# Attention with position bias and two feed-forward stages on one core: one pair of heads instead of two handled tile by tile right behind the bias rows

## The chip, the core and the metric

The kernel runs on one core of a Trainium2 chip. The metric is the time of one execution in microseconds (us) on the device. Five engines work side by side, each through its own instructions in order: TensorE (PE; its weight loads, PEld, are listed apart), VectorE (DVE), ScalarE (ACT), GpSimd (POOL) and SyncE (SP), whose queue issues nearly all DMA transfers.

## The reference

```python
scores = scale * np.matmul(q, k.transpose(0, 1, 3, 2))        # 4 batches, 8 heads, 576 tokens, head size 64
x = (np.log1p(np.abs(rel)) / psi_i)[..., None]                # rel: distance of two positions
bias = np.maximum(x @ w1 + b1, 0.0) @ w2                      # hidden size 32, one value per head
scores = scores + bias.transpose(2, 0, 1)[None]               # the same bias for every batch
attn = softmax(scores)
x = (attn @ v)                                                # to 2304 tokens x 512
h = x @ w_in; x = (P(h) / Q(h)) @ w_out                       # P, Q: polynomials; 2048 hidden
h = max(x @ w1, x @ w2, x @ w3); out = h @ w_out              # 768 hidden
```

## The kernel before, in words

The work has four stages: the bias rows, attention, and two feed-forward stages. Nearly all engines follow an order of instructions that is written out by hand (`ordered(3)` and the step list `A2` in the constants `KN`).

**Bias stage** (lines 1014 to 1037). The bias depends on the distance of two tokens, for each row divided by a number of that row. It is built in 36 groups of 16 rows: `bias_hidden` makes four hidden tiles of a group (ReLU of table plus column), each on ScalarE (line 189) or on VectorE (line 191); the list `H2` names the groups whose second hidden tile is ScalarE's. `bias_out` multiplies them on TensorE (line 215), evicts the sum on ScalarE (line 220) and stores it to DRAM (line 222). `bias_load` (lines 234 and 240 to 242) reads the rows back, skewed, for one tile of 128 query rows (t = 0 to 3, the last, t = 4, has 64) and one pair of heads (p = 0 to 3). SP's queue holds all these stores and loads in order.

In the same stage the first `FP` = 2 pairs of batch 0 are prepared: `split_kq` writes k and q as a high part and a remainder (fp32r), in six steps, placed by `SP0` behind given groups and run on VectorE. The k and q loads of pairs 0 and 1 are the first transfers of the kernel; those of pair 2 stand in the stage as well (`L0`). Bias rows of pairs below `FP` are loaded in this stage (the fifth tile's at position 2 of attention), those of the others four positions ahead of their use.

**Attention** (`attn_tick`, line 1130) works through a list of 80 units (batch, group of tiles, tile t, pair p). For a unit: scores on TensorE (line 268, or 279 for t = 4), a VectorE reduction that adds the bias and finds the maximum (line 294), exponentials with row sums on ScalarE (line 300); two positions later transposes on TensorE (lines 400, 406) and their evictions on ScalarE and VectorE (lines 1169, 421, 423); two more positions later the product with v (line 451), scaled by the reciprocal sums and stored.

The reciprocal sums take one of two ways. Pairs that are "own" (batch 0, p < `FP`) go tile by tile, in the order t0 p0, t0 p1, t1 p0, ...: each unit's sums are guarded (line 328, GpSimd), inverted (line 333, VectorE), spread over 64 columns (line 335, GpSimd) and transposed on TensorE with the unit's tiles (line 409). All other pairs go five units at a time, tiles [0, 1] and [2, 3, 4]; their sums are guarded once per group on ScalarE (line 326), inverted, and go through DRAM (lines 354 and 364). For pairs that are not own, `splits_at` puts the split's steps, two per position, on GpSimd, and `loads_at` their k and q loads. From position 10 on, feed-forward weights are brought in as well.

Of the kernel before, what the change touches and what calls it, by code (L numbers as in the profile page):

```python
# [17 lines left out]
P = 128  # L18
# [8 lines left out]
HID = 32  # L27
LR = 608
EW = S + 15
KN = {'PM': [0, 1, 2, 3, 4, 5, 6, 7, 8, 9, 10, 11, 12, 13, 14, 15, 16, 17, 18, 19, 20, 21, 22, 23, 24, 25, 26, 27, 28, 29, 30, 31, 32, 33, 34, 35], 'GD': 1, 'XS': 5, 'A3': ['na', 'T', 'v0', 'v1', 'av', 'n', 'st'], 'RL': 2, 'NSG': 4, 'RX': 2, 'AVL': 2, 'NSLOT': 35, 'NRAW': 3, 'NRAWX': 2, 'NATT': 4, 'HB': 0, 'NE': 'd', 'FP': 2, 'BL': 4, 'T4': 0, 'LSP': 1, 'KX': 2, 'HT': 'ss', 'EVP': 'da', 'TTP': 'dda', 'NXS': 5, 'EARLY': 4, 'NM0': 0, 'MAN': 3, 'MANF': 3, 'HA': 2, 'H0': [34, 35], 'L0': [(3, 'k2'), (6, 'v2')], 'B4': 2, 'H2': [1, 2, 4, 6, 8, 12], 'SP0': [3, 4], 'BW': 10, 'A2': ['na', 'sc', 'sq1', 'av', 'T', 'r0', 'r1', 'st', 'n', 'p1', 'p2', 'sq', 'e0', 'e1', 'v0', 'v1'], 'LL': 7, 'SL': 3, 'LL0': 9, 'SL0': 2, 'SQ': [1], 'CUT2': 1, 'CUT3': 4, 'WS': 14, 'WR': 41, 'EV': {None: 'da', 's': 'da', 'j': 'aa'}, 'WT': 64, 'XT': 8, 'XA': 3, 'XB': 8, 'F': ['g2a', 'g2d', 'h', 'g1a', 'w', 'g2p', 'g1d', 'g1p', 'y', 'x', 'g3'], 'LOW': 0, 'LOM': 3, 'LOI': 2, 'GHI': 'dve', 'GLO': 'dve', 'BED': 8, 'BE0': 16, 'NU1': 'pool', 'XE': ['act', 'pool'], 'RS': 3, 'PW': 1, 'WP': 10, 'NPK': 27, 'YSP': 'act', 'LAG': 2, 'EV1': 'dve', 'XSE': 'act', 'STQ': 'sp', 'PUQ': 'sp', 'NB0': 0, 'HP': 0, 'SB': 2, 'XLA': 3, 'XLB': 6, 'XSA': 11, 'YL': 4, 'MIX': [1, 2, 3], 'YN': [(6, 2), (6, 4), (6, 6), (7, 1), (7, 3), (7, 5), (8, 1), (8, 3), (8, 4), (8, 5)], 'WLOW': 1, 'YSN': {5: 2, 6: 2, 7: 1, 8: 1, 9: 1, 10: 1, 11: 1, 12: 1}, 'PLAN': [(2, 1, [0, 2, 3, 4, 5, 6, 7, 8]), (3, 1, [4, 6, 7, 8, 9, 10, 11, 12]), (4, 1, [8, 10, 11, 12, 13, 14, 15, 16]), (5, 2, [0, 2, 4, 5, 6, 8, 10, 12, 14]), (6, 3, [0, 2, 3, 4, 5, 6, 7, 8]), (7, 3, [4, 6, 7, 8, 9, 10, 11, 12]), (8, 3, [8, 10, 11, 12, 13, 14, 15, 16]), (0, 4, [0, 2, 3, 4, 5, 6, 7, 8]), (1, 4, [6, 8, 9, 10, 11, 12, 13, 14])], 'WPN': {13: 1, 14: 1, 15: 1}, 'OB': [1, 5]}  # L30
REBIAS = 2.0 ** -112
TOSIGN = -2.0 ** 32
QC = 1.0 + 1e-6
# [4 lines left out]
def tile_attention_moe(  # L38
# [7 lines left out]
    pe, act, dve, pool, sp = nc.tensor, nc.scalar, nc.vector, nc.gpsimd, nc.sync  # L46
# [5 lines left out]
    def slot(name, shape, dt):  # L52
        return sb.tile(shape, dt, tag="slot", name=name, bufs=KN['NSLOT'])

    def raw(name, shape, dt):
        return sb.tile(shape, dt, tag="raw", name=name, bufs=KN['NRAW'])

    def rawx(name, shape, dt):
        return sb.tile(shape, dt, tag="rawx", name=name, bufs=KN['NRAWX'])

# [34 lines left out]
    A0, A1, A2, A3 = (par[:, i:i + 1] for i in range(4))  # L95
# [206 lines left out]
    def own(b, p):  # L302
        return b == 0 and p < KN["FP"]
# [14 lines left out]
    def sum_guard(b, ts, t, p, eng=pool):  # L318
        if own(b, p):
            r = sums[b, t, p, 0]  # L320
        elif t == ts[-1]:
            r = sums[b, tuple(ts), p][0]
        else:
            return
        if eng is act:
            act.activation(r, r, AF.Identity, bias=eps)
        else:
            eng.tensor_scalar(r, r, 1e-9, 0.0, ALU.add, ALU.add)

    def sums_turn(b, ts, t, p):  # L330
        if own(b, p):
            r = sums.pop((b, t, p, 0))
            dve.reciprocal(r, r)
            rb = sb.tile([P, 512], F32, tag="xs", name=f"rb{b}_{t}_{p}", bufs=KN['NXS'])[:, :P].rearrange("p (u d) -> p u d", u=2)
            pool.tensor_copy(rb, r.unsqueeze(2).to_broadcast([P, 2, 64]))
            rbs[b, t, p] = rb
            return
        if t != ts[-1]:
            return
        sum_guard(b, ts, t, p, act)  # L340
        ts = tuple(ts)
        r_off.append((b, ts, p))
        r, sg = sums.pop((b, ts, p))
        dve.reciprocal(r, r)
        tr = sb.tile([P, 32], F32, tag="sgt", name=f"sgt{b}_{ts[0]}_{p}", bufs=3)
        dve.transpose(tr, sg)
        for n, t in enumerate(ts):
            for u in range(2):
                if t < 4:
                    rows = tr[2 * n + u:P:32, :]  # L350
                else:
                    rows = tr[64 * u + 2 * n:64 * u + 64:32, :]
                dst = r_d[b, p][u, t * P:min(S, (t + 1) * P)]
                r_due.append(lambda dst=dst, rows=rows: sp.dma_start(dst.rearrange("(c i) -> c i", i=32), rows))
# [609 lines left out]
    loads_at, splits_at, bloads_at = {}, {}, {}  # L964
# [4 lines left out]
    for i, (b, ts, t, p) in enumerate(units):  # L969
        if b == 0 and t == 4 and p < KN["FP"]:  # L970
            bloads_at.setdefault(KN["B4"], []).append((t, p))
        if t == 0 and (b > 0 or p >= KN["FP"]):
            lead, lag = (KN["LL0"], KN["SL0"]) if (b, p) == (0, KN["FP"]) else (KN["LL"] - 1, KN["SL"] - 1) if (b, p) == (1, 0) else (KN["LL"], KN["SL"] - 1) if b else (KN["LL"], KN["SL"])
            loads_at.setdefault(i - lead, []).append((b, p))
            splits_at.setdefault(i - lead + lag, []).append((b, p))
        if b == 0 and late(t, p):
            bloads_at.setdefault(i - KN["BL"], []).append((t, p))

# [151 lines left out]
    def attn_tick(n):  # L1130
# [7 lines left out]
        u1 = units[n - 1] if 1 <= n <= NU else None  # L1138
# [4 lines left out]
        for step in KN["A2"] if n <= NU else KN["A3"]:  # L1143
            if step == "sc" and u0:
                if u0[2] == u0[1][0]:
                    at_tiles(u0[0], u0[1], u0[3])
                    sums_begin(u0[0], tuple(u0[1]), u0[3])
                scores(u0[0], u0[2], u0[3])
            elif step in ("r0", "r1") and u0:
                reduce_min(u0[0], u0[2], u0[3], int(step[1]))  # L1150
                if step == "r1" and xlow and xlow[-1]:
                    xlow.pop()()
            elif step in ("e0", "e1") and u0 and (step == "e0" or u0[2] < 4):
                expo(u0[0], u0[2], u0[3], int(step[1]))
            elif step == "st":
                while stq:
                    attn_store(*stq.pop(0))
                stq.extend(st_next)
                st_next.clear()
            elif step == "T" and u2:  # L1160
                ev = transposes(u2[0], u2[2], u2[3], n >= NU)
            elif step == "na" and u1:
                if own(u1[0], u1[3]):
                    sum_guard(*u1)
            elif step == "n" and u1:
                sums_turn(*u1)
                tail_copy(u1[0], u1[2], u1[3])
            elif step == "v0" and u2:
                act.copy(*ev[0])  # L1169
            elif step == "v1" and u2:  # L1170
                for e_ in ev[1:len(ev) - 1]:
                    evac(evp, e_)
                evac(ttp, ev[-1])
            elif step == "p1":
                early_pop(kind)
            elif step == "av":
                if avq and avq[0][0] <= n:
                    _, av, js = avq.pop(0)
                    attn_v(*av, js)
                    if 4 in js:  # L1180
                        (st_next if len(av[1]) == 2 and not own(av[0], av[2]) else stq).append(av)
                if u2 and u2[2] == u2[1][-1]:
                    av = (u2[0], u2[1], u2[3])
                    cuts = {1: (5,), 2: (3, 2), 3: (2, 2, 1), 4: (4, 0, 1), 5: (5,)}
                    cut = {1: (5,), 2: cuts[KN["CUT2"]], 3: cuts[KN["CUT3"]]}[len(u2[1])]
                    avq.extend((n + KN["AVL"], av, range(sum(cut[:k]), sum(cut[:k + 1]))) for k in range(len(cut)))
            elif step == "sq1":
                for bp in splits_at.get(n, []):
                    sqq.extend(split_kq(*bp))
                if sqq:  # L1190
                    sqq.pop(0)()
            elif step == "sq":
                for _ in range(KN["SQ"][n % len(KN["SQ"])]):
                    if sqq:
                        sqq.pop(0)()
# [7 lines left out]
        WT, XT = KN["WT"], KN["XT"]  # L1203
# [13 lines left out]
    n = NU  # L1217
# [107 lines left out]
```

## Time and profile before

| what | us |
|---|---|
| median of three runs | 992.99 (992.95 to 995.52) |
| the profiled execution | 993.15 |
| its span, first to last instruction | 991.4 |
| bias stage, to the first scores | 53.5 |
| ten units of the two own pairs, to the third pair's first scores | 29.5 |
| busy: TensorE, VectorE, ScalarE, GpSimd | 976.3, 760.7, 636.7, 478.6 |

The granted TensorE clock is full throughout. Busy time of TensorE is counted with modelled ends of its matmuls, so weight loading (PEld) is the better sign of how full it is within a short stretch.

### The profile page before, as it was taken

To read this page: it belongs to the slowest core of one execution; us is meant where nothing else is said; L and a number is where in the kernel's file an instruction comes from. 1 tells how busy PE (TensorE), PEld (TensorE's weight loads), DVE (VectorE), ACT (ScalarE), POOL (GpSimd) and SP (SyncE) were. 2 spreads that over 40 slices of the span, in tenths; PEclk is the share of its full clock that TensorE was granted. 3 is DMA by queue.
4 is the path that set the end of the run, shared out by engine and by line. 5 is a ranking of instruction groups with operands and counts; after the bars stand their busy time and mean duration, and the time that the engine had idled before them with its cause. 6 is when DMAs were issued, how large, how long until landed. Compare 5 with 4: busy or idle time off the path is not lost. (4 is left out here: it accounts for less than half of the span.)

```text
span 991.4 us, 17489 instructions
## 1 busy us (share of the span) xinstructions
PE 976.3 (98%) x6076; PEld 813.0 (82%) x6076; DVE 760.7 (77%) x1466; ACT 636.7 (64%) x1319; POOL 478.6 (48%) x549
## 2 busy tenths in 40 slices
PE   6999999999999999999999999999999999999998
PEld 2389777787777788888898888887899999999997
DVE  8976787777687998988898888978696565666554
ACT  8977888888798888777788778788531211131111
POOL 4054766567572546256545356489431741371111
PEclk9999999999999999999999999999999999999999
DMA  8998686765662531223332332511597458655711
GB/s 312 320 301 268 237 280 208 265 221 205 191 217 92 184 102 43 75 85 138 104 121 97 116 127 96 181 61 60 198 388 249 159 192 285 225 172 200 256 32 64
DMA packets 76265, 176.69 MB, mean 178 GB/s; under 512 B 8848, under 2 KB 29968, under 8 KB 76176
## 3 DMA queue, kind: packets, MB, share of 16 engines
q1 hardware_dynamic: 76032, 175.27, 51.3%
q8 instruction: 48, 0.79, 0.3%
q14 instruction: 41, 0.34, 0.1%
q10 hardware_dynamic: 144, 0.29, 0.1%
HBM read 128.66 MB, written 46.87 MB: 177 GB/s over the span
## 5 line engine op out<-in xcount | busy, mean ns | idle before, releaser
L611 PE MATMUL y<-gs,wwo 128*128 128x512 f32 (+1 forms) x940 | 213.6, 373 | 1.1 <-POOL gs L669 0.6
L611 PE MATMUL ph<-xs,wwi 128*128 128x512 f32 (+1 forms) x930 | 205.6, 369 | 0.2
L611 PEld LDWEIGHTS y<-gs,wwo 128*128 128x128 f32 x940 | 164.2, 188 | 37.0 <-POOL gs L669 3.4
L611 PEld LDWEIGHTS ph<-xs,wwi 128*128 128x128 f32 x930 | 162.4, 188 | 32.9 <-issue 0.9
L897 PE MATMUL pr<-yo,ws 128*128 128x384 f32 x875 | 188.8, 335 | 0.4 <-ACT u L912 0.4
L669 POOL TENSOR_TENSOR gs<-gring,gs 128x512 fp32r<-128x512 f32 (+1 forms) x77 | 92.9, 1206 | 158.0 <-ACT gs L668 78.0
L897 PEld LDWEIGHTS pr<-yo,ws 128*128 128x128 f32 x875 | 155.5, 188 | 5.9 <-ACT u L912 0.7
L300 ACT ACTIVATE e<-e,st 128x576 f32<-128x576 f32 x144 | 110.9, 774 | 30.5 <-DVE st L294 29.2
L294 DVE CUSTOM_DVE_ANT_0 e<-s,bias 128x576 f32<-128x576 f32 x144 | 103.9, 752 | 27.3 <-PE s L268 13.8
L876 POOL TENSOR_TENSOR h<-m,h 128x384 fp32r<-128x384 f32 x36 | 36.5, 1015 | 157.3 <-ACT h L875 139.4
L642 ACT ACTIVATE s<-ph,keep 128x512 f32<-128x512 f32 (+1 forms) x80 | 49.5, 619 | 61.3 <-PE ph L611 60.8
L268 PE MATMUL s<-k,qs 128*128 128x288 f32 x512 | 84.8, 306 | 1.4 <-DVE st L294 0.5
L944 PE MATMUL o<-wmo,h 128*128 128x512 f32 x324 | 82.8, 393 | 0.0
L400 PE MATMUL tp<-ident,e 128*128 128x128 f32 x564 | 78.1, 279 | 0.2 <-ACT at L1169 0.2
L912 ACT COPY u<-pr 128x384 f32<-128x384 f32 x27 | 12.9, 478 | 101.4 <-PE pr L897 101.4
L400 PEld LDWEIGHTS tp<-ident,e 128*128 128x128 f32 x564 | 61.5, 141 | 19.4 <-issue 7.1
L268 PEld LDWEIGHTS s<-k,qs 128*128 128x128 f32 x512 | 70.1, 189 | 3.5 <-DVE st L294 1.8
L644 DVE SCALAR_TENSOR_TENSOR gring<-gring,keep,s 128x512 f32<-128x512 f32 (+1 forms) x77 | 53.0, 688 | 25.8 <-ACT gring L643 25.3
L451 PE MATMUL av<-at,v 128*64 128x320 f32 (+3 forms) x576 | 70.1, 385 | 0.0
L944 PEld LDWEIGHTS o<-wmo,h 128*128 128x128 f32 x324 | 60.1, 188 | 9.7
L875 ACT CAST h<-m 128x384 fp32r<-128x384 f32 x36 | 18.5, 514 | 70.7 <-DVE m L886 64.5
L656 DVE SCALAR_TENSOR_TENSOR gring<-gring,keep,s 128x512 f32<-128x512 f32 (+1 forms) x77 | 53.2, 691 | 11.8 <-ACT s L650 7.1
(174 smaller groups left out, 1862.1 us busy)
## 6 DMA issues: line engine op xcount, KB each, us to landing
ws<-ms_d SPq DMA_DIRECT2D x75, 512.0 KB
ms_d<-wring SPq DMA_DIRECT2D x21, 512.0 KB
bias_d<-bo SPq DMA_DIRECT2D x36, 295.5 KB
kr<-in_k SPq DMA_DIRECT2D x16, 576.0 KB
qr<-in_q SPq DMA_DIRECT2D x16, 576.0 KB
bias<-bias_d SPq DMA_DIRECT2D x16, 576.0 KB
nr<-in_m SPq DMA_DIRECT2D x18, 512.0 KB
wrwin<-in_wi SPq DMA_DIRECT2D x16, 512.0 KB
```

Source lines behind the costliest of these rows:

```text
L268: pe.matmul(pt[:, x, :HS], lhsT=qs[:, u, t * P:(t + 1) * P], rhs=ks[u][:, w, x * HS:(x + 1) * HS], start=w == 0, stop=w == 1,)
L294: dve.tensor_tensor_reduce(out=dst, in0=src, in1=bs, op0=ALU.add, op1=ALU.min, scale=-0.125, scalar=3.0e38, accum_out=st[:, u:u + 1],)
L300: act.activation(et[:, u], et[:, u], AF.Exp, bias=st[:, u:u + 1], scale=-1.0, accum_out=sums[b, t, p][u])
L400: pe.transpose(tp[:, j * P:(j + 1) * P], flat[:, 640 * u + j * P:640 * u + (j + 1) * P], ident)
L451: pe.matmul(po[r, :n], lhsT=l, rhs=m, start=j == 0, stop=j == 4, skip_group_check=True)
L611: pe.matmul(po, lhsT=wpart(key, a, k), rhs=rhs, start=first and i == 0, stop=last and i == 2)
L642: act.activation(s, ph, AF.Abs, scale=B0)
L644: dve.scalar_tensor_tensor(q, q, B1, s, ALU.mult, ALU.add)
L656: dve.scalar_tensor_tensor(u, u, A0, s, ALU.add, ALU.mult)
L669: (dve if blk == 0 and f < KN["GD"] else pool).tensor_tensor(t[1], u, f32(t[0]), ALU.subtract)
L897: pe.matmul(pt, lhsT=w[:, a, ch * P:ch * P + P], rhs=ys[c][ch], start=ch == 0 and i == 0, stop=ch == 1 and i == 2,)
L944: pe.matmul(po, lhsT=h[:, a, (tt % 3) * P:(tt % 3 + 1) * P], rhs=mo_t[j][:, c], start=j == 0 and i == 0, stop=j == NF2 - 1 and i == 2,)
```

## The change

`FP` goes from 2 to 1: only pair 0 of batch 0 is own, with units t0 to t4 of pair 0 first and pair 1 after it in groups [0, 1] and [2, 3, 4]. From this follows: VectorE no longer splits pair 1 in the bias stage (`SP0` has one entry); its split runs on GpSimd from position 0 on. Its bias rows are loaded four positions ahead of their use and no longer in the bias stage. Its sums go through DRAM. `H2` shrinks from six groups to three, so the second hidden tiles of groups 4, 8 and 12 pass from ScalarE to VectorE. For own units the guard and the spreading of the reciprocal pass from GpSimd to ScalarE. Pair 2's split keeps its place at position 3; pair 3's load moves from position 8 to 6 and its split from 11 to 9 (`LX`).

```diff
-KN = {... 'FP': 2, ... 'H2': [1, 2, 4, 6, 8, 12], 'SP0': [3, 4], ...}
+KN = {... 'FP': 1, ... 'H2': [1, 2, 6], 'SP0': [3], ... 'LX': 9}
...
-            pool.tensor_copy(rb, r.unsqueeze(2).to_broadcast([P, 2, 64]))
+            act.copy(rb, r.unsqueeze(2).to_broadcast([P, 2, 64]))
...
-            lead, lag = (KN["LL0"], KN["SL0"]) if (b, p) == (0, KN["FP"]) else (KN["LL"] - 1, KN["SL"] - 1) if (b, p) == (1, 0) else (KN["LL"], KN["SL"] - 1) if b else (KN["LL"], KN["SL"])
+            lead, lag = (KN["LL0"], KN["SL0"]) if (b, p) == (0, KN["FP"]) else (KN["LL"], 0) if (b, p) == (0, 2) else (KN["LX"], 3) if (b, p) == (0, 3) else (KN["LL"] - 1, KN["SL"] - 1) if (b, p) == (1, 0) else (KN["LL"], KN["SL"] - 1) if b else (KN["LL"], KN["SL"])
             loads_at.setdefault(i - lead, []).append((b, p))
-            splits_at.setdefault(i - lead + lag, []).append((b, p))
+            splits_at.setdefault(max(0, i - lead + lag), []).append((b, p))
...
                 if own(u1[0], u1[3]):
-                    sum_guard(*u1)
+                    sum_guard(*u1, act)
```

## Rows read from the trace of the kernel before

**Rows 1.** The page's engine totals: busy us, share of the span, instructions.
```profile
PE 976.3 (98%) x6076; PEld 813.0 (82%) x6076; DVE 760.7 (77%) x1466; ACT 636.7 (64%) x1319; POOL 478.6 (48%) x549
```
**Rows 2.** Busy time by stretch: stretch, length, busy per engine, clock, DMA share, GB/s.
```profile
0.00:53.40 53.40, 45.21 (x640) 17.25 (x640) 47.41 (x123) 47.12 (x77) 11.13 (x31) 1.00 0.91 322
53.40:65.10 11.70, 11.29 (x108) 9.88 (x98) 9.30 (x27) 10.57 (x26) 5.56 (x11) 1.00 0.93 337
65.10:83.00 17.90, 17.90 (x197) 16.46 (x196) 11.15 (x31) 11.20 (x27) 8.37 (x22) 1.00 0.88 265
...
128.60:144.30 15.70, 15.70 (x125) 12.52 (x124) 12.79 (x34) 13.49 (x35) 10.08 (x14) 1.00 0.82 271
```
**Rows 3.** Waits of weight loading, 10 to 53.4 us: total, times, longest.
```profile
PEld pb L215 <- ACT bo L220: 17.6, 29, 1.5
...
PEld pb L215 <- DVE h L191: 0.9, 4, 0.4
```
**Rows 4.** Timeline of the first positions: start, length, engine, line, instruction, count, idle before.
```profile
53.50 0.79 PE L268 MATMUL s<-k,qs 128*128 128x288 f32 x4
...
65.11 1.30 PE L268 MATMUL s<-k,qs 128*128 128x288 f32 x8
...
66.78 0.78 ACT L300 ACTIVATE e<-e,st 128x576 f32<-128x576 f32 x1 [1.02 <-DVE st L294]
...
83.01 1.30 PE L268 MATMUL s<-k,qs 128*128 128x288 f32 x8
```
**Rows 5.** Lines 147, 150, 141, 144 on VectorE: count, ns shortest/median/longest, starts, forms.
```profile
L147 DVE TENSOR_SCALAR k<-kr x4: 449/471/568, 10.8 to 12.8; 128x576 fp32r<-128x576 f32 x4
...
L150 DVE TENSOR_TENSOR k<-kr,k x4: 744/767/874, 14.5 to 19.5; 128x576 fp32r<-128x576 f32 x4
...
L141 DVE TENSOR_SCALAR qs<-qr x2: 679/680/681, 21.2 to 22.4; 128x1024 fp32r<-128x1024 f32 x2
...
L144 DVE TENSOR_TENSOR qs<-qr,qs x4: 689/689/690, 24.1 to 29.4; 64x512 fp32r<-64x512 f32 x4
```
**Rows 6.** Lines 189 and 191, the hidden tiles on ScalarE and on VectorE.
```profile
L189 ACT ACTIVATE h<-tab_sb,psi x39: 538/676/812, 5.1 to 48.7; 128x544 f32<-128x544 f32 x3, 128x512 f32<-128x512 f32 x3, 128x480 f32<-128x480 f32 x3, 128x448 f32<-128x448 f32 x3
...
L191 DVE TENSOR_SCALAR h<-tab_sb,psi x104: 370/432/528, 4.7 to 51.1; 128x576 f32<-128x576 f32 x7, 128x560 f32<-128x560 f32 x6, 128x528 f32<-128x528 f32 x6, 128x496 f32<-128x496 f32 x6
```
**Rows 7.** Timeline of the bias stage: two evictions with the idle time before them.
```profile
30.63 0.76 ACT L220 ACTIVATE bo<-pb,keep 128x591 f32<-128x591 f32 x1 [0.54 <-PE pb L215]
...
32.69 0.76 ACT L220 ACTIVATE bo<-pb,keep 128x591 f32<-128x591 f32 x1 [0.86 <-ACT h L189]
```
**Rows 8.** Lines 326, 333, 335, 409: the operations on the sums.
```profile
L326 ACT ACTIVATE sg<-sg,keep x5: 297/298/308, 89.6 to 121.0; 128x4 f32<-128x4 f32 x3, 128x5 f32<-128x5 f32 x2
...
L333 DVE RECIPROCAL so<-so x10: 152/158/168, 57.6 to 85.2; 128x2 f32<-128x2 f32 x8, 128x1 f32<-128x1 f32 x2
...
L335 POOL COPY rb<-so x10: 283/289/292, 57.9 to 85.5; 128x128 f32<-128x128 f32 x10
...
L409 PEld LDWEIGHTS tt<-ident,rb x10: 140/144/144, 59.3 to 86.4; 128*128 128x128 f32 x10
```
**Rows 9.** Timeline of GpSimd: an early tail of pair 0, and pair 2's split.
```profile
7.93 3.84 POOL L155 TENSOR_SCALAR qtail<-qr 128x64 fp32r<-128x64 f32 x1 [4.44 <-DMA qr<-in_q]
...
60.66 1.31 POOL L147 TENSOR_SCALAR k<-kr 128x576 fp32r<-128x576 f32 x2
...
66.61 0.24 POOL L155 TENSOR_SCALAR qtail<-qr 128x64 fp32r<-128x64 f32 x1
...
71.46 0.51 POOL L161 COPY vz<-v 64x64 f32<-64x64 f32 x2
```
**Rows 10.** Waits of SP's queue, 50 to 66 us: total, times, longest.
```profile
SPq L240 <- DMA bias_d<-bo: 4.8, 2, 4.0
```
**Rows 11.** Line 222, the stores of the bias rows, as in rows 5.
```profile
L222 SPq DMA_DIRECT2D bias_d<-bo x36: 315/320/456, 9.2 to 55.4; - x36
```
**Rows 12.** Timeline of SP: the first load of the fifth tile's bias rows.
```profile
62.42 0.70 SPq L240 DMA_DIRECT2D bias<-bias_d x1
```

More of the change, by code (lines that the diff above doesn't have):

```diff
@@ L29 @@
 EW = S + 15
-KN = {'PM': [0, 1, 2, 3, 4, 5, 6, 7, 8, 9, 10, 11, 12, 13, 14, 15, 16, 17, 18, 19, 20, 21, 22, 23, 24, 25, 26, 27, 28, 29, 30, 31, 32, 33, 34, 35], 'GD': 1, 'XS': 5, 'A3': ['na', 'T', 'v0', 'v1', 'av', 'n', 'st'], 'RL': 2, 'NSG': 4, 'RX': 2, 'AVL': 2, 'NSLOT': 35, 'NRAW': 3, 'NRAWX': 2, 'NATT': 4, 'HB': 0, 'NE': 'd', 'FP': 2, 'BL': 4, 'T4': 0, 'LSP': 1, 'KX': 2, 'HT': 'ss', 'EVP': 'da', 'TTP': 'dda', 'NXS': 5, 'EARLY': 4, 'NM0': 0, 'MAN': 3, 'MANF': 3, 'HA': 2, 'H0': [34, 35], 'L0': [(3, 'k2'), (6, 'v2')], 'B4': 2, 'H2': [1, 2, 4, 6, 8, 12], 'SP0': [3, 4], 'BW': 10, 'A2': ['na', 'sc', 'sq1', 'av', 'T', 'r0', 'r1', 'st', 'n', 'p1', 'p2', 'sq', 'e0', 'e1', 'v0', 'v1'], 'LL': 7, 'SL': 3, 'LL0': 9, 'SL0': 2, 'SQ': [1], 'CUT2': 1, 'CUT3': 4, 'WS': 14, 'WR': 41, 'EV': {None: 'da', 's': 'da', 'j': 'aa'}, 'WT': 64, 'XT': 8, 'XA': 3, 'XB': 8, 'F': ['g2a', 'g2d', 'h', 'g1a', 'w', 'g2p', 'g1d', 'g1p', 'y', 'x', 'g3'], 'LOW': 0, 'LOM': 3, 'LOI': 2, 'GHI': 'dve', 'GLO': 'dve', 'BED': 8, 'BE0': 16, 'NU1': 'pool', 'XE': ['act', 'pool'], 'RS': 3, 'PW': 1, 'WP': 10, 'NPK': 27, 'YSP': 'act', 'LAG': 2, 'EV1': 'dve', 'XSE': 'act', 'STQ': 'sp', 'PUQ': 'sp', 'NB0': 0, 'HP': 0, 'SB': 2, 'XLA': 3, 'XLB': 6, 'XSA': 11, 'YL': 4, 'MIX': [1, 2, 3], 'YN': [(6, 2), (6, 4), (6, 6), (7, 1), (7, 3), (7, 5), (8, 1), (8, 3), (8, 4), (8, 5)], 'WLOW': 1, 'YSN': {5: 2, 6: 2, 7: 1, 8: 1, 9: 1, 10: 1, 11: 1, 12: 1}, 'PLAN': [(2, 1, [0, 2, 3, 4, 5, 6, 7, 8]), (3, 1, [4, 6, 7, 8, 9, 10, 11, 12]), (4, 1, [8, 10, 11, 12, 13, 14, 15, 16]), (5, 2, [0, 2, 4, 5, 6, 8, 10, 12, 14]), (6, 3, [0, 2, 3, 4, 5, 6, 7, 8]), (7, 3, [4, 6, 7, 8, 9, 10, 11, 12]), (8, 3, [8, 10, 11, 12, 13, 14, 15, 16]), (0, 4, [0, 2, 3, 4, 5, 6, 7, 8]), (1, 4, [6, 8, 9, 10, 11, 12, 13, 14])], 'WPN': {13: 1, 14: 1, 15: 1}, 'OB': [1, 5]}
@@ new lines @@
+KN = {'PM': [0, 1, 2, 3, 4, 5, 6, 7, 8, 9, 10, 11, 12, 13, 14, 15, 16, 17, 18, 19, 20, 21, 22, 23, 24, 25, 26, 27, 28, 29, 30, 31, 32, 33, 34, 35], 'GD': 1, 'XS': 5, 'A3': ['na', 'T', 'v0', 'v1', 'av', 'n', 'st'], 'RL': 2, 'NSG': 4, 'RX': 2, 'AVL': 2, 'NSLOT': 35, 'NRAW': 3, 'NRAWX': 2, 'NATT': 4, 'HB': 0, 'NE': 'd', 'FP': 1, 'BL': 4, 'T4': 0, 'LSP': 1, 'KX': 2, 'HT': 'ss', 'EVP': 'da', 'TTP': 'dda', 'NXS': 5, 'EARLY': 4, 'NM0': 0, 'MAN': 3, 'MANF': 3, 'HA': 2, 'H0': [34, 35], 'L0': [(3, 'k2'), (6, 'v2')], 'B4': 2, 'H2': [1, 2, 6], 'SP0': [3], 'BW': 10, 'A2': ['na', 'sc', 'sq1', 'av', 'T', 'r0', 'r1', 'st', 'n', 'p1', 'p2', 'sq', 'e0', 'e1', 'v0', 'v1'], 'LL': 7, 'SL': 3, 'LL0': 9, 'SL0': 2, 'SQ': [1], 'CUT2': 1, 'CUT3': 4, 'WS': 14, 'WR': 41, 'EV': {None: 'da', 's': 'da', 'j': 'aa'}, 'WT': 64, 'XT': 8, 'XA': 3, 'XB': 8, 'F': ['g2a', 'g2d', 'h', 'g1a', 'w', 'g2p', 'g1d', 'g1p', 'y', 'x', 'g3'], 'LOW': 0, 'LOM': 3, 'LOI': 2, 'GHI': 'dve', 'GLO': 'dve', 'BED': 8, 'BE0': 16, 'NU1': 'pool', 'XE': ['act', 'pool'], 'RS': 3, 'PW': 1, 'WP': 10, 'NPK': 27, 'YSP': 'act', 'LAG': 2, 'EV1': 'dve', 'XSE': 'act', 'STQ': 'sp', 'PUQ': 'sp', 'NB0': 0, 'HP': 0, 'SB': 2, 'XLA': 3, 'XLB': 6, 'XSA': 11, 'YL': 4, 'MIX': [1, 2, 3], 'YN': [(6, 2), (6, 4), (6, 6), (7, 1), (7, 3), (7, 5), (8, 1), (8, 3), (8, 4), (8, 5)], 'WLOW': 1, 'YSN': {5: 2, 6: 2, 7: 1, 8: 1, 9: 1, 10: 1, 11: 1, 12: 1}, 'PLAN': [(2, 1, [0, 2, 3, 4, 5, 6, 7, 8]), (3, 1, [4, 6, 7, 8, 9, 10, 11, 12]), (4, 1, [8, 10, 11, 12, 13, 14, 15, 16]), (5, 2, [0, 2, 4, 5, 6, 8, 10, 12, 14]), (6, 3, [0, 2, 3, 4, 5, 6, 7, 8]), (7, 3, [4, 6, 7, 8, 9, 10, 11, 12]), (8, 3, [8, 10, 11, 12, 13, 14, 15, 16]), (0, 4, [0, 2, 3, 4, 5, 6, 7, 8]), (1, 4, [6, 8, 9, 10, 11, 12, 13, 14])], 'WPN': {13: 1, 14: 1, 15: 1}, 'OB': [1, 5], 'LX': 9}
```

## The prediction

> **What bounds the kernel now.** I read the page's engine totals first, then busy time by stretch, the waits inside the first stretch, and the timeline around the change. The reader is to see in the totals that TensorE is busy 976.3 of a span of 991.4 us [rows 1]: whatever the change does, it acts through the 15 us in which TensorE is idle, through TensorE's own work, or by letting new idle time in. The table by stretch says where that can be [rows 2]. From 128.6 to 144.3 us, one pair of heads in its settled state, TensorE is busy all 15.70 us. In the bias stage (up to 53.4 us) VectorE is busy 47.4 and ScalarE 47.1 of 53.4 us, but weight loading only 17.3: here the two vector engines set the pace, not TensorE. The waits of that stage agree: the weight loads waited 17.6 us for ScalarE's evictions and 0.9 us for VectorE [rows 3]. The next stretch, 53.4 to 65.1 us, the first five positions of attention, is the odd one: ScalarE is busy 10.57 of 11.70 us, more than weight loading (9.88) and VectorE (9.30). There ScalarE sets the pace; from 65.1 us on it has slack (11.20 of 17.90) and TensorE has none. So the change has two places to work in: the bias stage, where VectorE and ScalarE decide, and the first positions, where ScalarE decides.
>
> I count in "positions" (places in the list of units). Position 0 begins with the score products at 53.50 us, position 5 at 65.11 us [rows 4].
>
> **The bias stage: earlier by 3.1 us.** VectorE loses the second pair's split: two k highs at 0.471, two k lows at 0.767, one q high at 0.680 and two q lows at 0.689 us [rows 5], 4.5 us together. It gains three hidden tiles (groups 4, 8 and 12) at 0.432 each [rows 6], 1.3 us. Net 3.2 us less. ScalarE loses those three tiles, nominally 0.676 each [rows 6], 2.0 us; these groups are of the middle widths, somewhat below the median, so I take 1.9. It also waited 0.54 and 0.86 us before its evictions at 30.63 and 32.69 us [rows 7], just behind the last pieces of the second pair's split: VectorE was late with its hidden tiles there. These waits go: 1.4 us. So ScalarE's chain comes out 3.3 us shorter and VectorE's 3.2; after 33 us both run without gaps and are carried along unchanged. I take 3.1. The lower bound is 1.9 (only ScalarE's three tiles), the upper 3.3. A lower end of zero needs another bound on the stage, which is a rival below.
>
> **The first positions: later by 2.3 us.** With only one pair treated tile by tile, positions 0 to 4 are its five query tiles. For each, the guard of the sum and the broadcast of its reciprocal move from GpSimd to ScalarE. On GpSimd they were free. On ScalarE each position has a guard of 0.298 us (the same operation as line 326), a VectorE reciprocal of 0.158 us that ScalarE must wait for between the two, and a broadcast that I put at GpSimd's 0.289 us [rows 8]. That is 0.75 us in the stretch where ScalarE already ran without a gap: five times, 3.7 us. ScalarE is in order, so both exponentials and the evictions of the position queue behind the broadcast, and TensorE's transposes wait for the evictions (their PSUM banks). The first broadcast waits longer, because the reciprocal stands behind both reductions of the next tile on VectorE: e of position 1 begins after them and not between them, some 0.8 us more. Against this, ScalarE had 1.02 us of idle time before its exponential at 66.78 us [rows 4] and about 7 us in the 17.9 after 65.1 [rows 2], so the delay stops growing at position 4 and part is given back. 3.7 + 0.8 - 1.0 (idle at position 5), less some 1.2 that positions 6 and 7, which have neither guard nor broadcast, give back: 2.3. Bounds: 0, if all of it falls into waits, and 4.5, if none is given back.
>
> **TensorE's own work: 0.7 us less.** Five transposes of the broadcast reciprocals go, at 0.140 us of weight load each [rows 8]. The value products of the second pair cover the same 576 columns in two wide groups instead of four narrow ones; I cost this at nothing, and likewise the five reciprocals and evictions off TensorE's path. Bounds 0 and 0.9.
>
> **Edits that I cost at nothing, and their cover.** GpSimd splits the second pair: from its first k high at 60.66 us to its last copy at 71.97 us the third pair's split took 11.3 us, eight small operations of the tile-by-tile sums included [rows 9]. It can start at position 0 (about 50.4 us) and would end by 61.7; position 5 comes at 65.11 - 3.1 + 2.3 = 64.3 us. Slack 2.6 us; if the start is held until late bias tiles leave their buffers, it costs up to 3. The second pair's sums now go through DRAM (ten small stores and four loads more on SP's queue); its first product with them is at position 11, 15 us behind, and the third and fourth pair run like this already. The fourth pair's load, now at position 6, waits for GpSimd's split of the third; SP's queue is held behind it, with bias rows needed only four positions later.
>
> The bias rows are the tightest. Position 4, not 8, now reads the fifth tile's rows. Their load needs all bias stores to have ended: before, the last store was issued at 55.4 us and the load at 62.42, 7.0 us later, 4.0 of them SP waiting for just that [rows 10 to 12]. In those 7 us the engines also moved two 576 KB loads that are gone now or come later; at the 337 GB/s of this stretch [rows 2] one is 1.75 us. So I expect the load about 3.5 us behind the last store, at 52.3 + 3.5 = 55.8 us, behind one other 576 KB load (the second pair's first), and done 1.75 + 1.75 us plus some 2 us of issue and landing later, near 61.3. Position 4's first reduction would want it at about 61.9 with the delay of the part above. Cost 0, without slack; if the stores still take 7.0 us it comes 2.8 to 3 us late.
>
> **The sum.** 993.15 (the profiled execution, 1.75 us around its span) - 3.1 + 2.3 - 0.7 = 991.65. Its own time is 0.16 above the median of the runs shown, so 991.5.
>
> **Rivals.**
> 1. ScalarE's chain is absorbed: 993.15 - 3.1 - 0.7 = 989.35, less 0.16: 989.2. For it: ScalarE is idle 6.7 of the 17.9 us from 65.1 on. Against it: 53.4 to 65.1, where it is busy 90%.
> 2. The other side: the fifth tile's bias rows come late. The place is VectorE's reduction at position 4; behind it in order stand the reciprocal, so ScalarE's broadcast, exponentials and evictions, then TensorE's transposes. It decides once the load ends later than about 62 us; at 7.0 us behind the last store it costs 3: 994.5. For it: 0.93 of the DMA engines' time is used in that stretch and SP did wait 4.0 us. Against it: four 576 KB loads fewer ahead of it.
> 3. The bias stage doesn't shorten, because its DMA stores (0.91 of the engines' time [rows 2]) hold the buffers: 993.15 + 2.3 - 0.7 - 0.16 = 994.6. Against it: ScalarE and VectorE ran without gaps there.
> 4. GpSimd's split is late for position 5: 3 us, 994.5. One GpSimd operation on 64 columns took 3.84 us at 7.93 us, beside VectorE's stream of hidden tiles, where its like took 0.24 at 66.61 us [rows 9]. So a split that begins while that stream still runs gains little; the sum above counts from position 0, where the third pair's split took its 1.31 us for two k highs beside the reductions. The Trainium skill's "GPSIMD Engine Reference" (section 1, Specifications) says that GpSimd shares its SBUF interfaces with VectorE and contends with VectorE instructions in a two-port mode or with two SBUF inputs; by that rule the split would be slowed beside such instructions, and the 3.84 us agree with a hold of that kind, though no row here shows its cause.
>
> **How the numbers follow.** Forecast 0.50 (991.5; its own range 990.2 to 992.9), rival 1 0.25, rival 2 0.13, rival 3 0.07, rival 4 0.05. A measurement of this kernel tells 0.3%, 3.0 us, from no change. Faster than 990.0 takes most of rival 1 and the low edge of the forecast: 0.25. Slower than 996.0 needs two of the late cases together, or one larger than its bound: 0.08. The rest, 0.67, is within. The range reaches from rival 1's 989.2, with a little for a bias stage at its upper bound, to the three late cases: 988.8 to 994.8.
>
> **What would show it.** Right: position 0 near 50.4 us; ScalarE's guard and broadcast between the exponentials of positions 0 to 4, with the exponentials 3.4 us apart; position 5 near 64.3; the third pair's first scores near 80 instead of 83.01 us [rows 4] (1.5 us earlier, and 2 more of value products that are still owed); no wait of VectorE's reduction for a DMA at position 4; none of TensorE for GpSimd's q at position 5; from 130 us on the same rows shifted by 1 to 2 us. Wrong: position 0 later than 52 us (bias stage), a reduction waiting for bias rows (rival 2), ScalarE idle between guard and broadcast by more than 0.5 us, or a new stall after 100 us, where nothing of the change should reach.

## The result: 0.7% slower

After the change one execution takes 1000.34 us (median of six), before it 992.97 (median of six): a ratio of 1.007 [1.0058, 1.0081]. The forecast was 991.5, its range 988.8 to 994.8, and "slower" had a chance of 0.08. The prediction was wrong. One of the signs of error that it named itself came true: "a new stall after 100 us, where nothing of the change should reach". The profiled execution of after took 1000.69, with a span of 998.4, 7.0 more than before; its rows account for that.

The page's totals answer to [rows 1]: no engine has noticeably more work, so the 7 us are time in which TensorE waits or runs at a lower clock.

```profile
PE 976.2 (98%) x6031; PEld 810.2 (81%) x6031; DVE 755.7 (76%) x1459; ACT 637.2 (64%) x1328; POOL 475.8 (48%) x536
```

Where it waits is found by setting the starts of the positions against [rows 4] and the other score products of before. The timeline of TensorE after:

```profile
50.03 0.80 PE L268 MATMUL s<-k,qs 128*128 128x288 f32 x4
...
62.98 1.30 PE L268 MATMUL s<-k,qs 128*128 128x288 f32 x8
...
77.80 1.30 PE L268 MATMUL s<-k,qs 128*128 128x288 f32 x8
...
106.93 1.40 PE L279 MATMUL s<-k,qtail 128*128 128x288 f32 x10
...
114.77 2.57 PE L268 MATMUL s<-k,qs 128*128 128x288 f32 x8 [5.40 <-POOL qs L144]
...
119.62 1.30 PE L268 MATMUL s<-k,qs 128*128 128x288 f32 x8
```

| position | before | after | difference |
|---|---|---|---|
| 0 | 53.50 | 50.03 | -3.47 |
| 5 | 65.11 | 62.98 | -2.13 |
| 10 | 83.01 | 77.80 | -5.21 (part of it value products still owed) |
| 15 | 96.63 | 92.84 | -3.79 |
| 19 | 110.04 | 106.93 | -3.11 |
| 20 | 112.24 | 114.77 | +2.53 |
| 21 | 115.84 | 119.62 | +3.78 |
| 27 | 135.61 | 140.22 | +4.61 |
| 42 | 182.60 | 188.73 | +6.13 |

Position 47 adds 1.4 more; from there to the last position the difference stays between 7.0 and 7.6, and the spans end 7.0 apart. So the reader sees two things: up to position 19 the change gained more than the 1.5 us of the sum, and then, where batch 1 begins, TensorE stood still for 5.4 us. The waits of TensorE between 50 and 300 us (total, times, longest) name who it waited for; before had only 0.4 us for line 144 and none for line 375.

```profile
PE s L268 <- POOL qs L144: 5.4, 1, 5.4
PE tt L406 <- POOL e L375: 3.1, 3, 1.3
PE tt L406 <- ACT at L1169: 1.0, 1, 1.0
```

The busy times by stretch, columns as in [rows 2], show the bias stage and what the stop costs besides: the clock column falls to 0.50, and the eight score products at 114.77 take 2.57 us where eight take 1.30.

```profile
0.00:50.00 50.00, 43.51 (x640) 15.99 (x640) 43.85 (x119) 45.14 (x74) 9.56 (x28) 1.00 0.94 330
...
112.00:114.00 2.00, 0.00 (x0) 0.00 (x0) 0.00 (x0) 0.00 (x0) 1.75 (x6) 0.50 0.78 227
...
116.00:118.00 2.00, 2.00 (x9) 1.28 (x8) 1.39 (x3) 0.87 (x2) 0.46 (x2) 0.50 0.96 290
118.00:120.00 2.00, 2.00 (x16) 1.47 (x13) 1.15 (x6) 1.52 (x4) 1.57 (x4) 0.79 0.77 248
120.00:122.00 2.00, 2.00 (x19) 1.48 (x20) 2.00 (x6) 0.94 (x3) 2.00 (x2) 1.00 0.90 266
```

Why was line 144 late? It is the end of GpSimd's split of batch 1's first pair. GpSimd's timeline after (the bracket is the idle time before, and what ended it):

```profile
46.51 2.45 POOL L147 TENSOR_SCALAR k<-kr 128x576 fp32r<-128x576 f32 x2 [33.72 <-DMA bias_d<-bo]
...
56.64 0.51 POOL L161 COPY vz<-v 64x64 f32<-64x64 f32 x2
...
106.90 1.31 POOL L147 TENSOR_SCALAR k<-kr 128x576 fp32r<-128x576 f32 x2 [12.67 <-DMA kr<-in_k]
...
113.45 2.50 POOL L144 TENSOR_TENSOR qs<-qr,qs 64x512 fp32r<-64x512 f32 x2
...
138.60 1.31 POOL L147 TENSOR_SCALAR k<-kr 128x576 fp32r<-128x576 f32 x2 [9.84 <-DMA kr<-in_k]
139.85 0.23 POOL L375 COPY e<-e 128x64 f32<-128x64 f32 x1
```

And the same engine before:

```profile
103.43 1.74 POOL L147 TENSOR_SCALAR k<-kr 128x576 fp32r<-128x576 f32 x2 [5.51 <-DMA kr<-in_k]
...
131.86 1.56 POOL L147 TENSOR_SCALAR k<-kr 128x576 fp32r<-128x576 f32 x2 [5.93 <-PE tt L406]
```

GpSimd stood idle for 12.67 us for a k load: the engine was free, the data weren't there. It began at 106.90, 3.5 us later than before, while the scores that need the split were due 3.1 us earlier. The rows at 138.60 and 139.85 explain the later losses as well: GpSimd works in order, so the small copy of line 375, which TensorE's transposes need, stands behind a split that waits for its k. Before, the split of that place waited for TensorE and not for a transfer.

The last link is SP's queue, after:

```profile
61.33 0.34 SPq L128 DMA_DIRECT2D kr<-in_k  x1
67.43 0.34 SPq L130 DMA_DIRECT2D qr<-in_q  x1
...
71.26 0.33 SPq L128 DMA_DIRECT2D kr<-in_k  x1
...
73.11 2.76 SPq L354 DMA_DIRECT2D r_d<-sgt  x4
...
86.06 3.77 SPq L354 DMA_DIRECT2D r_d<-sgt  x6
...
100.46 0.43 SPq L128 DMA_DIRECT2D kr<-in_k  x1
```

and before:

```profile
96.18 0.43 SPq L128 DMA_DIRECT2D kr<-in_k  x1
```

Batch 1's first k was issued 4.3 us later. Three things stand ahead of it that weren't there: the second pair's sums (lines 354 and 364, 14 small transfers), three more loads of bias rows (line 234, 13 instead of 10: the second pair's, which stood in the bias stage before), and at 61.33 and 67.43 a k and q load that nothing should need. The issues by kind confirm the last; before it was x16:

```profile
kr<-in_k SPq DMA_DIRECT2D x17, 576.0 KB
```

The diff gives the third pair a lead of 7 and a lag of 0, so its load and its split fall on the same position, 3. The split's first step takes the raw tiles that the bias stage has loaded; the load at the end of the position no longer finds them and loads them again, for nothing. It costs the queue far more than its two issues: before the first SP stood 2.0 us until GpSimd had read the tile, before the second 5.7 us until the first had landed (waits of SP's queue, 58 to 72 us):

```profile
SPq L130 <- DMA kr<-in_k: 5.7, 1, 5.7
SPq L128 <- POOL k L150: 2.0, 1, 2.0
```

From position 0 to the v load of batch 1 (not counted), SP issued 52 transfers instead of 35, with 26.2 us of issue time instead of 17.8. The queue's own waits between 85 and 115 us say that its slack is gone. Before, the longest was for compute, that is, SP was ahead:

```profile
SPq L354 <- DVE sgt L346: 6.3, 1, 6.3
```

After, the longest are for transfers:

```profile
SPq L364 <- DMA r_d<-sgt: 2.5, 4, 1.4
...
SPq L459 <- DMA qr<-in_q: 0.9, 1, 0.9
```

How one transfer holds up another shows in the semaphores of the trace: every transfer of this program signals its landing on one of eight semaphores, which are taken in turn, and an issue stands until the transfer eight places ahead of it has landed. The wait for q in the last row is of this kind: the store of line 459 at 108.16 us stands eight places behind batch 1's q, issued at 100.93. So even a transfer of a few bytes takes a turn, and keeps it until it has landed.

### The profile page after: what moved, and what is told of

It reads as the page before. It is cut to its first block, busy times and chain, and to the rows that moved or that the text cites. A ratio compares the mean times of both kernels' runs of the same rounds, so it can differ in the third digit from the quotient of the medians.

```text
span 998.4 us, 17401 instructions
## 1 busy us (share of the span) xinstructions
PE 976.2 (98%) x6031; PEld 810.2 (81%) x6031; DVE 755.7 (76%) x1459; ACT 637.2 (64%) x1328; POOL 475.8 (48%) x536
## 5 line engine op out<-in xcount | busy, mean ns | idle before, releaser
L147 POOL TENSOR_SCALAR k<-kr 128x576 fp32r<-128x576 f32 x30 | 21.5, 733 | 111.6 <-DMA kr<-in_k 73.3
L644 DVE SCALAR_TENSOR_TENSOR gring<-gring,keep,s 128x512 f32<-128x512 f32 (+1 forms) x77 | 53.1, 689 | 25.2 <-ACT gring L643 24.8
```

What stands on the lines that cost most here:

```text
L644: dve.scalar_tensor_tensor(q, q, B1, s, ALU.mult, ALU.add)
```

## Experiments

Theory: the loss comes from transfers. SP's queue and the DMA engines get more to do ahead of batch 1's first k and q, and TensorE meets them where batch 1 begins. Rivals: only the double load counts; only the second pair's sums count; or ScalarE's guard and broadcast are the loss. No run takes away both the double load and the second pair's sums, and none tests the fourth pair's moved load by itself. Each run stands beside runs of the kernel before on the same chip.

**The double load alone, taken away and added.** The first kernel is the changed one with one load of the third pair, the second is the kernel before with a useless load at position 3.

```diff
+            if (b, p) != (0, 2):
                 loads_at.setdefault(i - lead, []).append((b, p))
```

> The changed kernel without the second load of the third pair's k and q at position 3 (the first, in the bias stage, stays). Theory D (this double load holds SP's queue until GpSimd has split the third pair, and the first load of batch 1 comes late from then on): SP issues that load near 92 to 96 us and not at 100.5, the wait of 5.4 us at position 20 falls below 1 us, TensorE keeps its full clock, and the time is 988 to 991 us. Theory S (the second pair's sums, ten stores and four loads more through SP's queue, make it late): the load is still issued after 98 us, and the time stays at 997 to 1000 us.

Measured: 997.25 against 992.37, ratio 1.0048 [1.0032, 1.0064]; the k of batch 1 issued at 98.6 instead of 100.46. TensorE's waits from 50 to 300 us:

```profile
PE s L268 <- POOL qs L144: 3.4, 2, 3.0
PE tt L406 <- POOL e L375: 1.7, 2, 1.1
PE tt L406 <- DVE xs L457: 1.5, 1, 1.5
```

```diff
+        if n == 3:
+            load_kq(0, 2)
         sums_flush()
```

> The kernel before, with the third pair's k and q loaded a second time at the end of position 3. Theory D: SP stands from about 61 us until GpSimd's split ends at 72 us, the first load of batch 1 is issued 3 to 5 us later than 96.2, and the time is 995 to 999 us. Theory S: the queue has room here, catches up before 96 us, and the time is 993 to 994 us.

Measured: 993.91 against 992.37, ratio 1.0019 [1.0005, 1.0032]. Each against the kernel before on its own chip, the double load is worth 2.5 us of the changed kernel's time (7.4 above it falls to 4.9) and 1.5 on the kernel before. In the latter batch 1's first k wasn't later (96.39); the loss stands behind late splits, at positions 27, 37 and 47. The profiled execution lies 3.8 us above this median, so its waits show the kind and not the size:

```profile
PE tt L406 <- POOL e L375: 3.5, 3, 1.8
```

So the double load counts, but some 4.9 of the 7.4 us are left without it.

**The second pair's sums.** The changed kernel, double load kept, with the second pair's sums tile by tile (no transfers through DRAM; guard and broadcast on ScalarE); and the kernel before with 14 tiny transfers (at most 4 KB) in SP's queue at positions 7 to 12, whose data nobody uses.

```diff
-        return b == 0 and p < KN["FP"]
+        return b == 0 and p < 2
```

> The changed kernel, double load kept, but the second pair's sums inverted and transposed tile by tile as the first pair's (no sums of it through DRAM; guard and broadcast on ScalarE for five more units). Theory D: the wait at position 20 stays above 3 us, 998 to 1002 us. Theory S: SP issues the first load of batch 1 near 94 us, the wait is gone, 990 to 993 us.

Measured: 997.39 against 992.37, ratio 1.0047 [1.0029, 1.0066]: 5.0 us above the kernel before instead of 7.4, which neither theory had. The wait for line 144 nearly goes (0.6 us), although batch 1's k is issued at 100.88, and another takes its place, so that TensorE is itself 3.9 us late at position 14: a broadcast of ScalarE waited for a store of `x_d`, which frees its buffer and stood in SP's queue behind the double load. ScalarE's timeline, and TensorE's waits:

```profile
74.70 0.30 ACT L335 COPY rb<-so 128x128 f32<-128x128 f32 x1 [4.24 <-DMA x_d<-xs]
```

```profile
PE tt L406 <- ACT at L1169: 4.7, 3, 3.5
```

```diff
+        for k in range({7: 4, 10: 6}.get(n, 0)):
+            sp.dma_start(fill_d[n // 10][k], ident[32 * (k % 4):32 * (k % 4) + 4, :32])
...
+        if n in (9, 12):
+            for k in range(2):
...
+                sp.dma_start(ft, src.unsqueeze(0).to_broadcast([64, 16]))
```

> The kernel before with 14 small transfers more in SP's queue at the places where the changed kernel has the second pair's sums (ten stores of 512 bytes at positions 7 and 10, four loads that read them at 9 and 12; nobody uses them). Theory Q: the first load of batch 1 is issued 3 to 7 us later than at 96.2 us, the wait for GpSimd's split at position 20 grows from 0.4 to 3 us or more, and the time is 996 to 999 us. If the queue has room: 992.5 to 993.5 us.

Measured: 994.12 against 992.22, ratio 1.0021 [1.001, 1.0031]. Fourteen transfers with next to no bytes cost 1.9 us. The profiled execution lies 3.6 us above this median, so its waits show the kind and not the size: k issued at 98.14 instead of 96.18, and

```profile
PE s L268 <- POOL qs L144: 3.3, 2, 2.9
```

**One transfer moved ahead.** Batch 1's first load three positions earlier, with and without the double load.

```diff
-... (KN["LL"] - 1, KN["SL"] - 1) if (b, p) == (1, 0) ...
+... (KN["LL"] + 2, KN["SL"] + 2) if (b, p) == (1, 0) ...
```

> The changed kernel, double load and sums kept, with the first k and q load of batch 1 at position 11 and not 14 (its split stays at position 16). Both theories say that it is this load's lateness that TensorE pays for: the wait at position 20 goes, about 6.5 us with the clock's fall behind it, and the time is 991 to 995 us, the later small waits (3 to 4 us) staying if SP's queue is still behind. If the load is not what matters, 1000 us.

> The changed kernel without the second load of the third pair and with the first k and q load of batch 1 at position 11 and not 14. Theory Q (SP's queue is full from position 5 on, with 14 more transfers of sums than before, at most eight of its transfers outstanding, so what stands late in it comes late; what matters is only where the k and q load stands): SP issues that load near 85 us, the 3.0 us wait of TensorE at position 20 and the half clock behind it go, some 4.5 us, and the time is 991 to 994 us, with small waits left from position 27 on. Theory D (the double load alone): no better than without it, 996 to 998 us.

Measured: with the double load 998.6 against 992.37, ratio 1.0062 [1.0043, 1.008]; without it 995.53 against 992.22, ratio 1.0039 [1.0023, 1.0055]. The wait for line 144 is gone in both, and the value products now wait for sums whose load stands behind k and q. The waits of the run with the double load (3.7 us in the one without):

```profile
PE av L451 <- DVE xs L457: 4.6, 1, 4.6
```

Whoever is moved ahead pushes another one back: the move brings only 1.1 us with the double load (7.4 above the kernel before falls to 6.2) and 1.6 without it (4.9 to 3.3).

**Another queue, and another engine.** The run without the double load with the second pair's 14 transfers issued from ScalarE's queue; and the run without it and with the earlier load, with guard and broadcast back on GpSimd.

```diff
-                r_due.append(lambda dst=dst, rows=rows: sp.dma_start(dst.rearrange("(c i) -> c i", i=32), rows))
+                r_due.append(lambda dst=dst, rows=rows, q=act if (b, p) == (0, 1) else sp: q.dma_start(dst.rearrange("(c i) -> c i", i=32), rows))
...
-            sp.dma_start(a2[r, 1, :n], src.unsqueeze(0).to_broadcast([64, n]))
+            (act if (b, p) == (0, 1) else sp).dma_start(a2[r, 1, :n], src.unsqueeze(0).to_broadcast([64, n]))
```

> The changed kernel without the second load of the third pair, and with the second pair's ten stores and four loads of sums issued from ScalarE's queue and not SP's. Theory Q: SP issues the first load of batch 1 near 93 us, the wait at position 20 falls below 1 us, and the time is 991 to 994 us (ScalarE gives some 0.5 us per issue, within its slack). Theory D: 996 to 998 us as without the double load.

Measured: 997.73 against 992.22, ratio 1.0053 [1.0037, 1.007], no better than 997.25; k still issued at 98.99. SP issued 36 transfers up to the v load, one more than before the change, and k was as late as without this edit. That doesn't clear SP's queue. The 14 transfers still take their turns on the same eight semaphores, and ScalarE, which works in order, now spends its time on issuing them: six stores took it 3.14 us, and the exponential behind them came 2.98 us late. SP for its part stood 6.1 us until bias rows had landed, and 3.1 for VectorE. ScalarE's timeline, and the longest of SP's waits from 85 to 115 us:

```profile
84.17 3.14 ACTq L354 DMA_DIRECT2D r_d<-sgt  x6
87.36 0.78 ACT L300 ACTIVATE e<-e,st 128x576 f32<-128x576 f32 x1 [2.98 <-DMA r_d<-sgt]
```

```profile
SPq L354 <- DMA bias<-bias_d: 6.6, 2, 6.1
```

The Trainium skill's "DMA: Bandwidth & Descriptors" (section Rules for kernel authors) says that spreading transfers over the issuing engines gives no bandwidth and saves only issue time. This run agrees on bandwidth: 261 GB/s between 50 and 100 us, against 260 in the run without the double load.

```diff
-            act.copy(rb, r.unsqueeze(2).to_broadcast([P, 2, 64]))
+            pool.tensor_copy(rb, r.unsqueeze(2).to_broadcast([P, 2, 64]))
...
-                    sum_guard(*u1, act)
+                    sum_guard(*u1)
```

> As e5_single_early, and the guard and the spreading of the first pair's reciprocals back on GpSimd. The prediction put 2.3 us on their move to ScalarE: then this is 1.5 to 2.5 us faster than e5_single_early. If ScalarE's chain costs nothing because position 4 waits for its bias rows anyway, or because GpSimd's two splits now stand in front of guard and spreading, it is the same or slower.

Measured: 998.59 against 992.22, ratio 1.0055 [1.0038, 1.0072], slower than its neighbour's 995.53. This doesn't price ScalarE's new work: on GpSimd the guards (line 328) now stand behind two splits, and VectorE's reciprocals wait for them (49 to 75 us):

```profile
DVE so L333 <- POOL so L328: 7.0, 4, 2.2
```

That ScalarE's new work isn't the loss is shown by the table of positions: from position 0 to 5, where that work stands, 1.3 us are lost, and none of it is left at position 15.

**Room in the stream.** The early feed-forward weights begin six positions later (512 KB loads that attention doesn't need; two of them stood ahead of batch 1's k), and with them ScalarE's and VectorE's work on these weights, in the changed kernel without the double load, in the kernel before, and in the changed kernel as it is.

```diff
-KN = {... 'WS': 14, 'WR': 41, ...}
+KN = {... 'WS': 20, 'WR': 46, ...}
```

> The changed kernel without the second load of the third pair, and with the early feed-forward weights begun at position 16 (work at 20, 46 steps in 48 positions) and not at 10 (14, 41 in 48). Theory M (the transfers of batch 0, some 31 MB, keep the DMA engines busy some 90% up to 104 us in every kernel; they end no earlier when compute gets ahead, so what the bias stage gains is lost where the first k and q of batch 1 are wanted): with some 3 MB of weights out of that stretch, k and q of batch 1 land before 101 us, no wait over 1 us at positions 16 to 21, and the time is 988.5 to 991.5 us. If the places in SP's queue alone decide: SP's queue loses only some eight transfers, the wait at position 20 stays above 1.5 us, and the time is 994 to 997 us.

> The kernel before with the early weights begun six positions later, as in e9_single_latew: the control for that edit. Both theories: the 0.7 us wait at position 20 goes, the rest is as before, 991.5 to 993 us.

> The changed kernel with the early weights begun six positions later and the double load kept. Theory M: the 1.2 MB of the double load stay in the stream but some 3 MB of weights leave it: most of the loss goes, 990 to 994 us. Theory D (SP standing in front of the double load sets the lag): 997 us or more.

Measured, all against 992.51: 993.21, ratio 1.0006 [0.9992, 1.002]; 991.3, ratio 0.999 [0.998, 0.9999]; 997.42, ratio 1.0047 [1.0032, 1.0062]. Room in the stream gives the changed kernel without the double load 4.2 us (4.9 above the kernel before falls to 0.7) and the one before 1.2 (992.51 to 991.3). The double load now costs 4.2 (993.21 to 997.42), as theory D had it and not theory M. In the first run neither theory's range was met. How much of its gain comes from the bytes, how much from the places and how much from the later work on the weights isn't separated.

Then the last late transfer: in the first of these, VectorE waited 4.5 us for the fifth tile's bias rows. The second pair's bias rows, which stood ahead of them, go one position later:

```diff
-            bloads_at.setdefault(i - KN["BL"], []).append((t, p))
+            bloads_at.setdefault(i - (KN["BL"] - 1 if p == 1 else KN["BL"]), []).append((t, p))
```

> As e9_single_latew, and the second pair's bias rows loaded three positions ahead and not four, so that the first of them stands behind the fifth tile's in SP's queue. If the reduction at position 4 waits because that 576 KB load stands in front (2.9 us of wait without the double load), this is 1 to 2 us faster than e9_single_latew; if the fifth tile's load is late because the bias stores end late, it is the same.

Measured: 991.03 against 992.51, ratio 0.9983 [0.9967, 1.0]. In this profile VectorE no longer waits for bias rows, k is issued at 96.00, and GpSimd has it at 102.17:

```profile
102.17 1.32 POOL L147 TENSOR_SCALAR k<-kr 128x576 fp32r<-128x576 f32 x2 [6.84 <-DMA kr<-in_k]
```

What is left of TensorE's waits:

```profile
PE tt L406 <- ACT at L1170: 1.0, 1, 1.0
PE tt L406 <- POOL e L375: 0.7, 1, 0.7
PE s L268 <- POOL qs L144: 0.4, 1, 0.4
```

Position 20 comes 2.33 us earlier than before the change. So three edits to transfers, one of which also moves the work on the weights, take the loss away. That the time is near the forecast (991.5) is luck: the later weights alone bring the kernel before to 991.3, and against that control the change gains 0.3 us, not 1.5.

**Is it faster than the kernel before?** The same kernel once more, weights still later (`'WS': 24, 'WR': 48`) in it, and that in the kernel before.

> e11_single_latew_bl once more, with more rounds: 990 to 992 us, 1 to 2 us below the kernel before, if the stream of transfers was what held the change back; 993 us or more if the first result was chance.

> As e11_single_latew_bl with the early weights begun at position 20 (work at 24, every position). If the waits at positions 27 to 47 come from the weights' transfers behind SP's late queue, they go and the time is 988.5 to 990.5 us; if from the new order of the pairs, it stays at 990.5 to 992 us.

> The kernel before with the early weights begun at position 20, the control for e13_latew24_bl: 990.5 to 992 us, as with position 16 (991.3), since its waits at positions 16 to 21 were already gone there.

Measured, all against 992.57: 991.03, ratio 0.999 [0.9978, 1.0002]; 992.11, ratio 0.9991 [0.998, 1.0003]; 992.67, ratio 1.0001 [0.999, 1.0012]. Still later weights bring nothing. The repaired change and the kernel before with later weights (991.3) lie 0.3 us apart, less than these intervals can tell: what the change of pairs adds to the later weights can't be told from nothing. In the second profile of the repaired kernel position 20 comes 3.59 us earlier than before the change. Part of that goes again in the same way: it loses 1.25 us between positions 52 and 57 (the first profile 0.92 between 42 and 47), where TensorE waits 1.1 (0.7) us for line 375.

## Why the prediction was wrong, step by step

**The bias stage: right.** -3.47 measured, -3.1 forecast; position 0 came at 50.03, forecast 50.4. The twelve profiles of kernels with this bias stage have position 0 between 2.6 and 3.6 us earlier. The busy times fell as forecast too: ScalarE's by 2.0 us (47.12 to 45.14; forecast 1.9), VectorE's by 3.6 (47.41 to 43.85; 3.2). With that rival 3 is out.

**ScalarE's chain: the mechanism right, the size too large.** From position 0 to 5 the gain shrank by 1.34 us, forecast 2.3. The first exponentials of positions 0 to 4 begin at 51.78, 54.61, 56.99, 59.99 and 63.81, 2.4 to 3.8 us apart, where 3.4 was forecast. ScalarE's timeline has guard and broadcast at the prices taken (0.30 each):

```profile
53.58 0.30 ACT L326 ACTIVATE so<-so,keep 128x2 f32<-128x2 f32 x1
54.40 0.30 ACT L335 COPY rb<-so 128x128 f32<-128x128 f32 x1 [0.53 <-DVE so L333]
...
63.61 0.30 ACT L335 COPY rb<-so 128x128 f32<-128x128 f32 x1 [1.06 <-DVE so L333]
```

The last one waited 1.06 us because VectorE was behind; that is rival 2, in small. Its reduction at position 4 did wait for the fifth tile's bias rows, 2.19 us of the 3 that rival 2 had priced:

```profile
62.53 0.76 DVE L294 CUSTOM_DVE_ANT_0 e<-s,bias 128x576 f32<-128x576 f32 x1 [2.19 <-DMA bias<-bias_d]
```

That wait cost TensorE next to nothing: from position 4 to 5 it lost 0.09 us. The repaired kernel lost 1.74 us from position 0 to 5 in its first profile, without such a wait (2.77 us ahead at position 0, 1.03 at position 5), and 1.34 in its second, with 0.9 at most. So the term was 0.6 to 1.0 too large.

**TensorE's own work: right in sign, too small.** Of the 45 instructions that are gone, five are the transposes of the reciprocals and 40 are value products (line 451: 680 instead of 720), which the prediction had put at nothing; weight loading is 2.8 us less in all. From position 5 to 15 the gain grew by 1.66 us, above the bound of 0.9; what the fewer products and what their order do in it isn't separated. From position 0 to 15 together the gain grew by 0.32 us, where the sum had it shrink by 1.6. So the kernel stood 3.79 us ahead there, at the 3.8 of rival 1, but not for rival 1's reason: ScalarE's chain did cost, and TensorE won it back.

**Rival 4: wrong.** GpSimd split the second pair from 46.51 to about 57 us, in the bias stage already, at 2.45 us for the two k highs instead of 1.31; it was done six us before position 5. The 3.84 us of [rows 9] that this rival leaned on is no fixed price: the same operation took 0.55 us in the trace of after, and 0.52 in that of the kernel before with the double load, whose bias stage is that of the kernel before.

**The step that failed: "Edits that I cost at nothing, and their cover".** At position 19 the kernel was 3.1 us ahead, more than the 1.5 that the sum asked for. Then what had been put at zero came: the second pair's sums through DRAM, its bias rows, and a load that the prediction didn't see although the diff shows it (lead 7, lag 0). Each transfer had been held against its own deadline ("its first product with them is at position 11, 15 us behind"), and the sums did meet theirs. The prediction even had SP's queue held behind a k load, and weighed that against bias rows alone. Not counted was whom it delays: k and q of batch 1, further back in the same queue. The chain from SP over GpSimd to TensorE had no slack at position 20 even before the change, and the trace of before says so in TensorE's waits:

```profile
PE s L268 <- POOL qs L144: 0.4, 1, 0.4
```

TensorE waited there for GpSimd, and GpSimd (the row at 103.43) for its k.

A second assumption lay under it: that a gain of compute is carried on to the end. It can't be carried past a point where the transfers set the time. The busy times of the first 104 us of after end in DMA share and GB/s:

```profile
0.00:104.00 104.00, 95.96 (x1079) 60.47 (x1081) 81.58 (x225) 88.28 (x190) 35.30 (x67) 1.00 0.90 303
```

and those of before:

```profile
0.00:104.00 104.00, 95.41 (x1103) 62.08 (x1104) 83.28 (x224) 85.15 (x170) 35.72 (x81) 1.00 0.89 305
```

The transfers moved no faster although the engines were some 3 us ahead. If batch 1's k comes when it came before, a gain of 3 us ends in a wait of 3 us at position 20; only a k that comes earlier carries it on, as in the second profile of the repaired kernel, where k is issued at 94.20 instead of 96.18 and position 20 comes 3.59 us earlier. The loss is 5.64 us from position 19 to 20, 1.25 at half the clock, 0.83, 1.52 and 1.40 at positions 27, 42 and 47; -3.11 plus these is +7.53, of which 7.0 are left at the end.

Taken in the order of the runs, the 7.4 us above the kernel before fall to 4.9 without the double load, to 0.7 with later weights, and to 1.5 below it with the bias rows one position later: steps of 2.5, 4.2 and 2.2 us, each known to some 2 us. Of the 4.2 the kernel before gains 1.2 as well. The sizes hang on the order (with later weights the double load costs 4.2): each is late only because of the others. What stays open is how much of the cost is turns in the queue (14 tiny transfers cost the kernel before 1.9 us) and how much the DMA engines' own time: an issue waits for a landing eight places ahead, so the two act together, and no run here separates them.

## What to carry to other kernels

An edit that shortens an engine's work gains only up to the next place where a transfer sets the time; look for that place in the waits of before (here an idle GpSimd waiting for its k, and a TensorE wait of 0.4 us) and price there. A transfer in an in-order queue isn't costed by its own deadline but by the transfers behind it, so count the issues between the edit and the next tight load, before and after. And when lead times are moved, follow each load to the split that uses it: the number of loads of a tensor in the two kernels (17 against 16) shows in one row what the diff hides.

## What the runs showed of the hardware

After a wait of 5.40 us TensorE's granted clock was 0.50 (1.2 GHz) in the rows up to 118 us, 0.79 in the next, and full (2.4 GHz) from 120 on; eight score products took 2.57 us instead of 1.30, and the position 1.25 us more: a stop costs more than its length. Fourteen transfers of at most 4 KB made the kernel before 1.9 us slower. This program's transfers use eight semaphores in turn, on both queues, and an issue waits for the landing eight places ahead. And GpSimd's two k highs beside VectorE's stream in the bias stage took 2.45 us, and in three other runs with the same stage 2.88, 1.68 and 1.42, against 1.31 elsewhere: slower, by no fixed factor.
